# Copies of the key tail on ScalarE, and maxima joined from PSUM and kept positive

## The chip, the cores and the metric

One Trainium2 chip, one core of it. The metric is the device time of one execution in microseconds (us). Three runs of the kernel before gave 593.42, 593.97 and 594.81 us, median 593.97 us.

## What is computed

Attention over 4 batches with 8 heads of 576 tokens and 64 columns, with rotary embedding, then a soft mixture of experts on the result, then a dense layer pair. Only the attention matters here:

```python
q_rot, k_rot = (rotate(q), rotate(k))
scale = 1.0 / np.sqrt(D)
scores = scale * np.matmul(q_rot, k_rot.transpose(0, 1, 3, 2))
scores = scores - np.max(scores, axis=-1, keepdims=True)
attn = np.exp(scores)
attn = attn / (np.sum(attn, axis=-1, keepdims=True) + 1e-09)
return np.matmul(attn, v).astype(np.float32)
```

## The kernel before

The 32 heads are worked in 16 pairs, two heads of a pair on the two halves of the 128 partitions. For a pair, rotated k and q are split into a rounded part `hi` (ScalarE, L374) and a rest `lo` (GpSimd, L344), so that products of rounded numbers on TensorE can be added up to full precision. Keys go in four units of 128 and one last unit of 64 keys; the queries go in two halves of 288.

Each pair takes these steps. **Rotation** (`rope_pair`, L344) runs on GpSimd, six operations of 128x576, and on VectorE for the first pair alone. **Parts** (`parts_pair`): L374 and L344 again. **Windows** (`windows`, L418 and L422): the columns of the last 64 keys are copied from `hi` and `lo` into `wins`, so that the two query halves can share one 128-wide unit (`BOTH`). **Maxima** (`max_unit`): TensorE multiplies the rounded parts (L438) into a PSUM bank pair, VectorE takes the row maxima (L449); nine units a pair. **Joining** (`max_rows`): VectorE joins the unit maxima (L460), TensorE transposes them into PSUM (L465), VectorE writes them negated into the small tile `mr` in SBUF (L471), joins the two halves of `mr` in place (L476), and SP sends two rows by DMA into `mrows`. **Scores** (`st_unit`): TensorE adds three products of the parts (L504) and then the maxima, spread by the constant matrix `pick` (L511); ScalarE takes the exponential (L523); GpSimd adds two units (L531). **Values** (`pv_unit`): L551 and L546. **Sums** (`norm`): TensorE L572, then VectorE L578 to L596. **Logits** (`logits`): L638, L615, L620, with copies on ScalarE (L643, L650) and VectorE (L627, L629).

The steps of neighbouring pairs are interleaved: the maxima of pair p+1 are worked while the scores of pair p are. The order on each engine is made at build time by `Plan.emit`: each `op` has a due time, a cost per engine (the dictionary that comes first, as `{"DVE": 0.2}`), what it reads and writes, and the planner places the most urgent operation that can start. The engines then run their queues in that order, whatever the real durations are.

The maxima, scores, sums, logits and the transposed joined maxima all use one ring of three PSUM bank pairs (`bank_89`, `bank_90`, `bank_91` in listings of the order). An operation with `take="ring"` gets the bank pair that was freed longest ago; the one with `give="ring"` (made by `ring_op`) frees it. So TensorE can be at most three such steps ahead of VectorE and ScalarE. Before the change it is L471 that gives back the bank of the joined maxima.

`Plan.emit` also puts filler matmuls (L1524) where it expects TensorE to idle long; ten of them stand at the start, behind the first maxima.

After the attention come the experts and the dense pair; from about 377 us on TensorE works L1453 without a break.

Of the kernel before, what the change touches and what calls it, by code (L numbers as in the profile page):

```python
# [14 lines left out]
AF = mybir.ActivationFunctionType  # L15
ALU = mybir.AluOpType
# [3 lines left out]
B, H, S, D = 4, 8, 576, 64  # L20


T = dict(
    cpd=-10.26, wph=-19.05, wi0b=-82.9, wi1=0.41,
    wi2=15.39, wi3=-0.78, wp=-10.16, wp0=-1.88, wo0=0, wo1=7.84, wo=6.08, ahead=2.82, WAIT=0.51,
    lod=5.12, b0=1, nwarm=8, sprope=0.8, mxpe=1.14, mxdve=-0.4, stpe=0.22, stact=0.68, sums=-2.36, mrdve=1.0, smm=-0.48,
    norm=4.2, rope=-22.0, parts=-20.0, v=-5.6, lag=7.5, mr0=0.0, lgt=5.5, slots=6.0,
)
# [165 lines left out]
def kernel(  # L194
# [14 lines left out]
    nc = tc.nc  # L209
    plan = Plan()  # L210
    op = plan.op
# [8 lines left out]
    HQ = S // 2  # L220
# [7 lines left out]
    pick = pool.tile([128, 256], F32R, name="pick")  # L228
# [22 lines left out]
    keep_apart = pool.tile([10, 32], F32, name="keep_apart")[:, 0:1]  # L251
# [31 lines left out]
    def f(ap):  # L283
        return ap.bitcast(F32)
# [13 lines left out]
    def dma(fn, due, kb, reads=(), writes=(), after=None, on="SP", behind=None):  # L298
        return op({on: 0.5}, lambda e: fn(), due, reads, writes, kb=kb, after=after, behind=behind)


    def setup():
        nc.gpsimd.memset(ones, 1.0)
        nc.scalar.activation(out=nms[0], in_=ones[:, 0:1], func=AF.Exp)
        nc.gpsimd.memset(es, 0.0)
        nc.gpsimd.memset(f(pick), 0.0)
        for j in range(2):
            nc.gpsimd.memset(f(pick)[64 * j : 64 * j + 1, 64:192], 1.0)
        for h in his:
            nc.vector.memset(f(h)[:, :, S:], 0.0)  # L310
        for m in mrows:
            nc.vector.memset(f(m), 0.0)
        for x in los:
            nc.vector.memset(f(x[0])[:, S:], 0.0)
        nc.gpsimd.memset(f(wins), 0.0)
        nc.gpsimd.memset(half_ones, 0.0)
        for i in range(2):
            nc.gpsimd.memset(half_ones[64 * i : 64 * i + 64, i], 1.0)
            mcol, _ = small("mcol", [128, 2, 2, 5], bufs=2)
            nc.gpsimd.memset(mcol[:, 1, :, 4], -3e38)  # L320
# [81 lines left out]
    def on_ring(tok):  # L402
        return PAIRS[tok["slot"]]

    def ring_op(*args, **kw):
        i = op(*args, **kw)
        ring_ops.add(i)
        return i
# [4 lines left out]
    def windows(p, g):  # L413

        to = wins[:, 384 * (p % 2) : 384 * (p % 2) + 384].rearrange("p (i z n) -> p i z n", i=3, z=2)[:, :, 1]
        hi, lo = his[p % NHI], los[p % NLO][0]
        op(
            {"DVE": 0.2}, lambda e: nc.vector.tensor_copy(out=to[:, 0:2], in_=f(hi)[:, :, 512:S]),  # L418
            g, [("hi", p % NHI, t) for t in range(2)], [("win", p % 2, 0)],
        )  # L420
        op(
            {"DVE": 0.15}, lambda e: nc.vector.tensor_copy(out=to[:, 2], in_=f(lo)[:, 512:S]),  # L422
            g + 0.1, [("lo", p % NLO, 0)], [("win", p % 2, 1)],
        )

# [27 lines left out]
    def max_rows(p, g):  # L453
        mr, mrk = small("mrow", [10, 128], F32R, bufs=2)
        m10, m10k = small("m10", [128, 10])
        mcol, mk = mcols[p]
        tok = {}
        op(
            {"DVE": 0.15},
            lambda e: nc.vector.tensor_reduce(out=m10, in_=mcol.rearrange("p h j u -> p (j u) h"), op=ALU.max, axis=AX.X),  # L460
            g + T["mrdve"], [(mk, u, h) for u in range(5) for h in range(2 if u < BOTH else 1)], [m10k],
        )
        op(
            {"PE": 0.11},
            lambda e: nc.tensor.transpose(on_ring(tok)[0:10, 0, 0:128], m10, ident),  # L465
            g, [m10k, "ident"], [("rw", p)], take="ring", tok=tok, mode="f",
        )

        ring_op(
            {"DVE": 0.25},  # L470
            lambda e: nc.vector.tensor_scalar(out=mr, in0=on_ring(tok)[0:10, 0, 0:128], scalar1=-1.0, scalar2=None, op0=ALU.mult),  # L471
            g + T["mrdve"], [("rw", p)], [mrk], give="ring", tok=tok,
        )
        op(
            {"DVE": 0.2},
            lambda e: nc.vector.scalar_tensor_tensor(  # L476
                out=mr[:, 0:64], in0=f(mr)[:, 64:128], scalar=keep_apart, in1=f(mr)[:, 0:64], op0=ALU.add, op1=ALU.min
            ),
            g + T["mrdve"], ["apart"], [mrk],
        )  # L480
        for j in range(2):
            rows_done[p] = dma(
                lambda j=j: nc.sync.dma_start(out=f(mrows[p % 2])[64 * j : 64 * j + 1, :], in_=f(mr)[5 * j : 5 * j + 5, :]),
                g, 3, [mrk], [("mrow", p % 2, j)],
            )
# [71 lines left out]
    def norm(p, h, g):  # L557


        n = (2 * p + h) % 2  # L560
        acc, rest = accs[n], [p_slot(p, h, u) for u in (2, 3, BOTH)]
        tok = {}
        QUAD = [slice(32 * i, 32 * i + 32) for i in range(4)]

        def sums(e):
            sm = on_ring(tok)[:, 0]
            xs_ = [acc] + [x for x, _ in rest]
            for i in range(2):
                for j in range(2):
                    for w in range(2):  # L570
                        one = half_ones[:, h] if i and w else ones[:, 0:32]
                        nc.tensor.matmul(  # L572
                            sm[QUAD[2 * j + w], 0:HQ], lhsT=one, rhs=xs_[2 * i + w][:, j, :], start=(i == 0), stop=(i == 1)
                        )

        op({"PE": 0.97}, sums, g + T["sums"], [("acc", n)] + [k for _, k in rest], [("sm", n)], take="ring", tok=tok, mode="q")
        op(
            {"DVE": 0.42}, lambda e: nc.vector.transpose(out=on_ring(tok)[:, 1, 0:HQ], in_=on_ring(tok)[:, 0, 0:HQ]),  # L578
            g, [], [("sm", n)],
        )  # L580

        def inverse(e):
            col = on_ring(tok)[:, 1, 0:HQ].rearrange("p (b c) -> p b c", c=32)[:, :, 0:1]
            nc.vector.tensor_scalar(out=r9, in0=col, scalar1=1e-9, scalar2=None, op0=ALU.add)
            for q in range(4):
                nc.vector.tensor_tensor(out=r9[QUAD[q]], in0=r9[QUAD[q]], in1=col[QUAD[q ^ 1]], op=ALU.add)
            nc.vector.reciprocal(out=r9, in_=r9)

        ring_op({"DVE": 1.0}, inverse, g, [("sm", n)], ["r9"], give="ring", tok=tok)
        op(  # L590
            {"DVE": 0.42}, lambda e: nc.vector.transpose(out=recT, in_=r9.to_broadcast([128, HQ // 32, 32])),
            g, ["r9"], ["recT"],
        )
        op(
            {"DVE": 0.38},
            lambda e: nc.vector.tensor_tensor(out=xT[:, HALF[h]], in0=BANKS[6 + h][:, 0:HQ], in1=recT, op=ALU.mult),  # L596
            g, [("O", h), "recT"], [("xT", h)],
        )
# [200 lines left out]
    ring = {}  # L799
# [110 lines left out]
    def first_loads():  # L910
        for n, (what, s) in enumerate((("kq", 0), ("k", 1), ("rope", 0), ("rope", 1), ("k", 2), ("rope", 2), ("q", 1), ("q", 2))):
            rows, to, of = SEGS[s]
            q = "ACT" if s else "SP"
            if what == "rope":
                dst, src, keys = rope_sb[rows, :, to], rope[:, rows, of].rearrange("t r c -> r t c"), [("rope", t, s) for t in range(2)]
            else:
                ts_ = {"kq": slice(0, 4), "k": slice(0, 4, 2), "q": slice(1, 4, 2)}[what]
                dst, src, keys = raws[0][rows, ts_, to], qk[0][rows, ts_, of], [("raw", 0, t, s) for t in range(4)[ts_]]
            done = dma(
                lambda dst=dst, src=src, q=q: QUEUE[q].dma_start(out=dst, in_=src),  # L920
                -99 + 0.01 * n, (500 if what != "kq" else 1000) * (to.stop - to.start) / S, (), keys, on=q,
            )
        load(1, -35.5, slice(0, 4), "ACT", after=done, first="ACT")
        dma(lambda: nc.sync.dma_start(out=ident, in_=ident_in), -34, 65, (), ["ident"])

        def apart(e):
            nc.vector.tensor_tensor(out=keep_apart, in0=ident[0:10, 4:5], in1=ident[0:10, 9:10], op=ALU.add)
            nc.vector.tensor_scalar(out=keep_apart, in0=keep_apart, scalar1=-3e38, scalar2=3e38, op0=ALU.mult, op1=ALU.add)

        op({"DVE": 0.3}, apart, -20, ["ident"], ["apart"])  # L930

# [681 lines left out]
```

## Time and profile before

| what | value |
|---|---|
| median of three runs | 593.97 us |
| time of the profiled execution | 592.18 us |
| its span, first to last instruction | 590.4 us |
| TensorE (PE) busy | 562.1 us, 95% |
| VectorE (DVE) busy | 406.6 us, 69% |
| ScalarE (ACT) busy | 269.5 us, 46% |
| GpSimd (POOL) busy | 217.5 us, 37% |
| mean granted TensorE clock | 0.994 of full speed |

The profiled execution lies 1.8 us below the median of the runs; 1.78 us of its time lie outside of its span. PE's weight loads (PEld) run beside its matmuls, and its busy time is modelled from the starts. A row of a timeline is a start, a duration, the engine, the line, the operation, the tiles (written before `<-`, read after it) and how many; in brackets the idle time of the engine before it and what ended that.

### The profile page before, as it was taken

The page shows a single profiled execution, that of the slowest core. Times are in us where ns is not written, and L with a number is a line of the kernel's source. Part 1 is how long each engine was busy: PE and PEld are TensorE (multiplying, and loading weights), DVE is VectorE, ACT ScalarE, POOL GpSimd, SP SyncE. Part 2 cuts the span into 40 slices and gives each one's busy share as a digit, 9 for nine tenths or more (in the row PEclk, how much of TensorE's full clock was granted, in tenths as well). Part 3 has the DMA queues.
Part 4 walks back from the last instruction along what each step waited for, and adds up shares of the span by engine and source line. Part 5 has one row for each costly group of instructions (what it writes and reads, how often), then busy time and mean ns, then how long its engine had stood idle before and what let it go on. Part 6 is the DMA issues. An engine that isn't in the chain of part 4 may idle for free.

```text
span 590.4 us, 13397 instructions
## 1 busy us (share of the span) xinstructions
PE 562.1 (95%) x5519; PEld 423.3 (72%) x5519; DVE 406.6 (69%) x853; ACT 269.5 (46%) x475; POOL 217.5 (37%) x172
## 2 busy tenths in 40 slices
PE   1899999999999999999999899999999999999996
PEld 1756565566665666666754337999999999999996
DVE  3687887887787787777455458995594587535553
ACT  1234444444444443453432237876864465443440
POOL 1999999986879677721200000000000000000000
PEclk9799999999999999999999999999999999999999
DMA  9556775566367244036469998421400120000222
GB/s 188 120 124 164 185 193 148 152 175 169 100 174 210 54 100 105 24 95 227 154 226 378 386 392 330 143 81 64 144 1 1 60 84 2 1 1 1 108 108 107
DMA packets 36253, 80.90 MB, mean 137 GB/s; under 512 B 7616, under 2 KB 8032, under 8 KB 35168
## 3 DMA queue, kind: packets, MB, share of 16 engines
q1 hardware_dynamic: 34704, 77.98, 43.2%
q10 hardware_dynamic: 1488, 2.06, 1.8%
q8 instruction: 43, 0.70, 0.5%
q14 instruction: 18, 0.15, 0.1%
HBM read 75.24 MB, written 4.72 MB: 135 GB/s over the span
## 4 chain that ended last, share of the span: by engine, by line
PE 81%; DVE 11%; issue 2%; ACT 2%; DMA 1%; POOL 1%; ACTq 0%; DVEq 0%
PE bank L1453 32%; PE obank L551 11%; PE bank L504 10%; PE bank L572 5%; DVE mcol L449 5%; PE bank L438 4%; PE bank L511 3%; PE obank L1385 3%; PE bank L1239 2%; PE bank L638 2%; PE obank L546 2%; DMA arena<-in_rope_dram 1%; PE bank L1178 1%; PE bank L615 1%; POOL arena L344 1%
## 5 line engine op out<-in xcount | busy, mean ns | idle before, releaser
L523 ACT ACTIVATE tO<-bank 128x576 f32<-128x576 f32 x144 | 90.7, 650 | 114.3 <-PE bank L511 87.3
L344 POOL TENSOR_TENSOR arena<-arena 128x576 f32<-128x576 f32 x90 | 125.6, 1418 | 6.8 <-DMA arena<-in_qk_dram 6.2
L449 DVE TENSOR_REDUCE mcol<-bank 128x2 f32<-128x576 f32 x144 | 103.6, 747 | 14.5 <-PE bank L438 12.3
L1453 PE MATMUL bank<-w,tEb 128*128 128x256 f32 x864 | 106.1, 279 | 0.1
L1453 PEld LDWEIGHTS bank<-w,tEb 128*128 128x128 f32 x864 | 103.3, 188 | 2.3 <-issue 1.2
L551 PE MATMUL obank<-tO,pb 128*64 128x288 f32 x512 | 82.2, 424 | 0.0
L531 POOL TENSOR_TENSOR pb<-tO 128x576 f32<-128x576 f32 x32 | 45.2, 1413 | 51.0 <-ACT tO L523 50.9
L1453 PE MATMUL bank<-w,tEa 128*128 128x256 f32 x432 | 53.5, 279 | 0.0
L1453 PEld LDWEIGHTS bank<-w,tEa 128*128 128x128 f32 x432 | 51.9, 188 | 1.2 <-issue 0.8
L1453 PE MATMUL bank<-w,tO 128*128 128x256 f32 x432 | 51.3, 276 | 0.0
L1453 PEld LDWEIGHTS bank<-w,tO 128*128 128x128 f32 x432 | 50.9, 188 | 0.0
L551 PEld LDWEIGHTS obank<-tO,pb 128*64 128x64 f32 x512 | 28.6, 135 | 26.1 <-issue 16.9
L1396 ACT ACTIVATE pb<-obank 128x384 f32<-128x384 f32 x47 | 21.7, 493 | 42.9 <-PE obank L1385 42.9
L1396 ACT ACTIVATE arena<-obank 128x384 f32<-128x384 f32 x48 | 21.7, 494 | 36.2 <-PE obank L1385 36.1
L572 PE MATMUL bank<-tO,ones 128*32 128x288 f32 x256 | 36.5, 409 | 0.0
L504 PE MATMUL bank<-tEb 64*128 64x288 f32 x180 | 30.8, 339 | 1.4 <-DVE mcol L449 1.4
L438 PE MATMUL bank<-tEb 64*128 64x288 f32 x180 | 27.9, 337 | 2.4 <-DVE mcol L449 2.4
L344 POOL TENSOR_TENSOR tLb<-arena,tEb 128x576 fp32r<-128x576 f32 x20 | 28.2, 1420 | 3.1 <-ACT tEb L374 2.9
L504 PEld LDWEIGHTS bank<-tEb 64*128 64x128 f32 x180 | 16.9, 185 | 16.3 <-ACT tO L523 4.8
L1385 PE MATMUL obank<-x,tO 128*128 128x384 f32 x95 | 27.6, 345 | 0.8 <-DVE tO L1333 0.4
L578 DVE STREAM_TRANSPOSE bank<-bank 128x288 f32<-128x288 f32 x32 | 15.9, 498 | 17.5 <-PE bank L572 17.4
L438 PEld LDWEIGHTS bank<-tEb 64*128 64x128 f32 x180 | 15.8, 184 | 16.4 <-issue 8.6
(302 smaller groups left out, 1066.1 us busy)
## 6 DMA issues: line engine op xcount, KB each, us to landing
arena<-in_qk_dram SPq DMA_DIRECT2D x15, 576.0 KB
arena<-in_qk_dram SPq DMA_DIRECT2D x14, 512.0 KB
pb<-in_v_dram SPq DMA_DIRECT2D x16, 320.0 KB
arena<-in_w_dram SPq DMA_DIRECT2D x8, 512.0 KB
tLb<-in_w_in_dram SPq DMA_DIRECT2D x3, 1024.0 KB
pb<-in_w_in_dram SPq DMA_DIRECT2D x3, 1024.0 KB
w__440<-in_w_dram SPq DMA_DIRECT2D x4, 512.0 KB
w__652<-in_w_dram SPq DMA_DIRECT2D x4, 512.0 KB
```

Of the source, the lines that this page charges most:

```text
L344: ENG[e].tensor_tensor(out=o, in0=x, in1=y, op=how)
L438: nc.tensor.matmul(on_ring(tok)[:, j, 0:HQ], lhsT=x[rows], rhs=hi[rows, 0, HALF[c]], start=(u < BOTH or c == 0), stop=(u < BOTH or c == 1),)
L449: lambda e: nc.vector.tensor_reduce(out=mcol[:, h, :, u], in_=on_ring(tok)[:, :, 0:HQ], op=ALU.max, axis=AX.X),
L504: nc.tensor.matmul(st[:, j, 0:HQ], lhsT=w[rows], rhs=q[y][rows, HALF[c]], start=(i == 0 and (u < BOTH or c == 0)), stop=False,)
L511: nc.tensor.matmul(st[:, j, 0:HQ], lhsT=pick[rows, w : w + 128], rhs=mrow[rows, HALF[c]], start=False, stop=(u < BOTH or c == 1),)
L523: lambda e: nc.scalar.activation(out=pr, in_=on_ring(tok)[:, :, 0:HQ], func=AF.Exp, scale=0.125),
L531: lambda e: nc.gpsimd.tensor_tensor(out=acc, in0=one, in1=pr, op=ALU.add),
L551: nc.tensor.matmul(BANKS[6 + h][o, 0:HQ], lhsT=vr[:, u, j, :], rhs=pr[:, j, :], start=(h == 0 and u == 0), stop=(h == 1 and u == 3))
L572: nc.tensor.matmul(sm[QUAD[2 * j + w], 0:HQ], lhsT=one, rhs=xs_[2 * i + w][:, j, :], start=(i == 0), stop=(i == 1))
L1385: lambda e, i=i, t0=t0: nc.tensor.matmul(BANKS[i][:, 0:384], lhsT=wst_of()[:, 128 * fc : 128 * fc + 128], rhs=cst_of()[:, t0 : t0 + 384], ...
L1396: lambda e, i=i, h=h: nc.scalar.activation(out=rg_of()[:, 0, h], in_=BANKS[i][:, 0:384], func=AF.Relu),
L1453: nc.tensor.matmul(BANKS[c][:, z], lhsT=gt[:, x, 128 * c : 128 * c + 128], rhs=wo[:, fc % 2, y, z], start=(fc % FQ == 0 and i == 0 and z.s ...
```

## The change

Four edits, all in the attention:

1. The two copies of `windows` (L418, L422) go from VectorE to ScalarE, as activations with the function Copy.
2. In `max_rows`, L471 copies the transposed maxima times 1.0 where it was times -1.0, and L476 takes its first input from the PSUM bank where it was the SBUF tile `mr`; it joins by the larger (max) where it was by the smaller (min).
3. The bank of the joined maxima is given back by L476 where it was by L471.
4. Signs that follow: `pick` holds -1.0 where it was 1.0, and `keep_apart` swaps its two constants. The planner's cost of L578 is 0.45 where it was 0.42.

```diff
-            nc.gpsimd.memset(f(pick)[64 * j : 64 * j + 1, 64:192], 1.0)
+            nc.gpsimd.memset(f(pick)[64 * j : 64 * j + 1, 64:192], -1.0)
...
-            {"DVE": 0.2}, lambda e: nc.vector.tensor_copy(out=to[:, 0:2], in_=f(hi)[:, :, 512:S]),
+            {"ACT": 0.22}, lambda e: nc.scalar.activation(out=to[:, 0:2], in_=f(hi)[:, :, 512:S], func=AF.Copy),
...
-            {"DVE": 0.15}, lambda e: nc.vector.tensor_copy(out=to[:, 2], in_=f(lo)[:, 512:S]),
+            {"ACT": 0.18}, lambda e: nc.scalar.activation(out=to[:, 2], in_=f(lo)[:, 512:S], func=AF.Copy),
...
+        op(
+            {"DVE": 0.25},
+            lambda e: nc.vector.tensor_scalar(out=mr, in0=on_ring(tok)[0:10, 0, 0:128], scalar1=1.0, scalar2=None, op0=ALU.mult),
+            g + T["mrdve"], [("rw", p)], [mrk],
+        )
         ring_op(
-            {"DVE": 0.25},
-            lambda e: nc.vector.tensor_scalar(out=mr, in0=on_ring(tok)[0:10, 0, 0:128], scalar1=-1.0, scalar2=None, op0=ALU.mult),
-            g + T["mrdve"], [("rw", p)], [mrk], give="ring", tok=tok,
-        )
-        op(
             {"DVE": 0.2},
             lambda e: nc.vector.scalar_tensor_tensor(
-                out=mr[:, 0:64], in0=f(mr)[:, 64:128], scalar=keep_apart, in1=f(mr)[:, 0:64], op0=ALU.add, op1=ALU.min
+                out=mr[:, 0:64], in0=on_ring(tok)[0:10, 0, 64:128], scalar=keep_apart, in1=f(mr)[:, 0:64], op0=ALU.add, op1=ALU.max
             ),
-            g + T["mrdve"], ["apart"], [mrk],
+            g + T["mrdve"], ["apart", ("rw", p)], [mrk], give="ring", tok=tok,
         )
...
-            {"DVE": 0.42}, lambda e: nc.vector.transpose(out=on_ring(tok)[:, 1, 0:HQ], in_=on_ring(tok)[:, 0, 0:HQ]),
+            {"DVE": 0.45}, lambda e: nc.vector.transpose(out=on_ring(tok)[:, 1, 0:HQ], in_=on_ring(tok)[:, 0, 0:HQ]),
...
-            nc.vector.tensor_scalar(out=keep_apart, in0=keep_apart, scalar1=-3e38, scalar2=3e38, op0=ALU.mult, op1=ALU.add)
+            nc.vector.tensor_scalar(out=keep_apart, in0=keep_apart, scalar1=3e38, scalar2=-3e38, op0=ALU.mult, op1=ALU.add)
```

The planner orders the engines anew. With the bank numbers left out, TensorE's order stays as it was but for one stretch in the maxima of the second pair, where one block of four value matmuls is parted into two blocks of two; the whole attention has 237 runs of one kind of matmul where it had 235. GpSimd's order and SP's stay, and behind the attention everything does. What changes is at which of the three banks a step lands, and VectorE's and ScalarE's queues.

VectorE in the third pair's maxima, behind the first pair's reciprocal. Before:

```order
L587 RECIPROCAL r_87<-r_87 128x9
L449 TENSOR_REDUCE mcol_113<-bank_91 128x2
L449 TENSOR_REDUCE mcol_113<-bank_89 128x2
L449 TENSOR_REDUCE mcol_113<-bank_90 128x2
L418 CAST wins<-tEb 128x2x64
L449 TENSOR_REDUCE mcol_113<-bank_91 128x2
L591 STREAM_TRANSPOSE pb<-r_87 128x288
L596 TENSOR_TENSOR pb<-obank_92,pb 128x288
```

Of the change:

```order
L587 RECIPROCAL r_87<-r_87 128x9
L449 TENSOR_REDUCE mcol_113<-bank_89 128x2
L449 TENSOR_REDUCE mcol_113<-bank_91 128x2
L449 TENSOR_REDUCE mcol_113<-bank_90 128x2
L449 TENSOR_REDUCE mcol_113<-bank_89 128x2
L591 STREAM_TRANSPOSE pb<-r_87 128x288
L596 TENSOR_TENSOR pb<-obank_92,pb 128x288
```

The copy between the third and the fourth reduction is gone, and the four stand one behind the other.

ScalarE in the scores of a pair of the first batch (L523 are the exponentials, L643 and L650 copies of the logits step). Before:

```order
L523 ACTIVATE tO_81<-bank_91 128x576
L523 ACTIVATE tO_81<-bank_89 128x576
L523 ACTIVATE tO_81<-bank_90 128x576
L523 ACTIVATE tO_82<-bank_91 128x576 x2
L523 ACTIVATE tO_82<-bank_90 128x576
L643 ACTIVATE arena<-bank_89 128x4x128
```

Of the change:

```order
L523 ACTIVATE tO_81<-bank_91 128x576
L523 ACTIVATE tO_81<-bank_90 128x576
L523 ACTIVATE tO_82<-bank_89 128x576
L418 ACTIVATE wins<-tEb 128x2x64
L422 ACTIVATE wins<-tLb 128x64
L523 ACTIVATE tO_82<-bank_89 128x576
L523 ACTIVATE tO_82<-bank_90 128x576
L643 ACTIVATE arena<-bank_91 128x4x128
```

Both copies stand between two exponentials of the same pair.

TensorE from the transposed joined maxima (L465) to the next step on the same bank, in the seventh pair, of the change:

```order
L465 MATMUL bank_90<-ident,m_119 10x128
L638 MATMUL bank_89<-ident,pb 128x128 x4
L638 MATMUL bank_89<-ident,pb 64x128
L615 MATMUL bank_91<-pb,phi_sb 32x128 x4
L620 MATMUL bank_91<-pb,phi_sb 32x64 x4
L572 MATMUL bank_90<-pb,ones 32x288
```

Before it is the same row by row, with L638 on `bank_91` and L615 and L620 on `bank_89`: two steps stand between L465 and the sums L572, which take the bank that the joining gives back. VectorE's side of it, of the change (before, L476 reads `mrow_120` twice and not the bank):

```order
L460 TENSOR_REDUCE m_119<-mcol_116 128x10
L449 TENSOR_REDUCE mcol_113<-bank_89 128x2
L471 TENSOR_SCALAR mrow_120<-bank_90 10x128
L476 SCALAR_TENSOR_TENSOR mrow_120<-bank_90,keep_apart,mrow_120 10x64
```

The bank is free for L572 behind L476 where it was behind L471.

## Rows read from the trace of the kernel before

**Rows 1.** Busy time by stretches: start:end, length, busy us and instructions of each engine.
```profile
100.00:150.00 50.00, 49.40 (x572) 30.50 (x569) 40.96 (x102) 21.88 (x41) 41.50 (x31) 1.00 0.61 156
320.00:345.00 25.00, 23.03 (x192) 8.38 (x188) 10.70 (x45) 6.43 (x15) 0.00 (x0) 1.00 1.05 389
```

**Rows 2.** Waits of PE, 45 to 285 us: waiter <- waited for: total us, times, longest.
```profile
PE bank L438 <- DVE mcol L449: 1.5, 2, 1.1
PE bank L504 <- DVE mcol L449: 1.3, 6, 0.3
PE bank L638 <- DVE mcol L449: 0.6, 2, 0.3
PE bank L504 <- ACT tO L523: 0.2, 1, 0.2
```

**Rows 3.** Timeline, DVE and PE: one wait of PE and what stands before it.
```profile
69.35 1.40 DVE L422 CAST wins<-tLb 128x64 fp32r<-128x64 f32 x1
70.67 1.41 DVE L449 TENSOR_REDUCE mcol<-bank 128x2 f32<-128x576 f32 x2
71.57 0.40 PE L438 MATMUL bank<-tEb 64*128 64x288 f32 x2 [0.40 <-DVE mcol L449]
```

**Rows 4.** Timeline, POOL, DVE and PE around the joined maxima of the seventh pair.
```profile
128.00 1.41 POOL L531 TENSOR_TENSOR pb<-tO 128x576 f32<-128x576 f32 x1 [0.88 <-ACT tO L523]
128.11 0.28 DVE L471 TENSOR_SCALAR mrow<-bank 10x128 fp32r<-10x128 f32 x1 [0.19 <-PE bank L465]
128.42 1.07 DVE L476 SCALAR_TENSOR_TENSOR mrow<-mrow,keep_apart 10x64 fp32r<-10x64 f32 x1
129.02 0.41 PE L572 MATMUL bank<-pb,ones 128*32 128x288 f32 x1
```

**Rows 5.** Groups by line: shapes, count | busy us, mean ns | idle before.
```profile
L418 DVE CAST wins<-tEb 128x128 fp32r<-128x128 f32 x10 | 7.4, 743 | 4.3 <-ACT tEb L374 2.2 <-PE bank L504 2.1
L418 DVE CAST wins<-tEa 128x128 fp32r<-128x128 f32 x6 | 2.1, 356 | 0.9 <-ACT tEa L374 0.8
L422 DVE CAST wins<-tLb 128x64 fp32r<-128x64 f32 x10 | 7.4, 741 | 2.1 <-POOL tLb L344 2.1
L422 DVE CAST wins<-tLa 128x64 fp32r<-128x64 f32 x6 | 3.2, 534 | 0.0
L476 DVE SCALAR_TENSOR_TENSOR mrow<-mrow,keep_apart 10x64 fp32r<-10x64 f32 x16 | 15.0, 940 | 0.6
```

**Rows 6.** Timeline, PE: a maxima step and the scores behind it, without and with a wait.
```profile
121.36 0.29 PE L438 MATMUL bank<-tEa 64*128 64x288 f32 x2
121.56 0.40 PE L504 MATMUL bank<-tEb 64*128 64x288 f32 x2
...
125.84 0.33 PE L438 MATMUL bank<-tEb 64*128 64x288 f32 x2
126.43 0.40 PE L504 MATMUL bank<-tEb 64*128 64x288 f32 x2 [0.26 <-DVE mcol L449]
```

**Rows 7.** Timeline, PE: fillers and first scores at the start; a wait at 43.77.
```profile
23.63 3.20 PE L1524 MATMUL obank<-es 128*128 128x128 f32 x14
26.76 0.58 PE L504 MATMUL bank<-tEa 64*128 64x288 f32 x2
43.77 0.40 PE L438 MATMUL bank<-tEb 64*128 64x288 f32 x2 [0.88 <-DVE mcol L449]
```

**Rows 8.** One line's durations, min/median/max ns, first and last start.
```profile
L476 DVE SCALAR_TENSOR_TENSOR mrow<-mrow,keep_apart x16: 273/1064/1176, 24.2 to 283.7; 10x64 fp32r<-10x64 f32 x16
L596 DVE TENSOR_TENSOR pb<-obank,pb x32: 440/447/459, 47.4 to 303.5; 128x288 f32<-128x288 f32 x32
L650 ACT ACTIVATE arena<-bank x8: 257/258/258, 59.5 to 249.2; 64x128 f32<-64x128 f32 x8
```

**Rows 9.** Waits of the whole span.
```profile
ACT tO L523 <- PE bank L511: 87.3, 71, 3.9
PEld obank L551 <- issue: 16.9, 80, 0.4
```

## The prediction

> **What bounds the kernel now.** I read the busy time by stretches first. In the middle of the attention TensorE is busy 49.40 of 50 us and VectorE 40.96 [rows 1]. So TensorE is the bound, and whatever the change does to VectorE is worth only what TensorE idles for VectorE's sake. Next I read what PE waits for between 45 and 285 us, where the pairs run in their steady order: ten waits for the maxima's reduction L449, 1.5 + 1.3 + 0.6 = 3.4 us, and a single one of 0.2 us for an exponential [rows 2]. That is the whole of PE's idle time that another engine causes there. Then the timeline, for what stands before such a wait: at 69.35 a copy L422 of 64 columns takes 1.40 us on VectorE, two reductions follow, and PE, which has all three banks out, gets one back only at 71.57 and has idled 0.40 us [rows 3]. The reader should see that the copy is long, not that VectorE is full. Last, why it is long: L476, on only ten partitions, takes anything from 0.273 to 1.176 us with a median of 1.064 [rows 8], and the one at 128.42 ends at 129.49, 0.08 us behind the end of a GpSimd operation that began before it (128.00 + 1.41 = 129.41) [rows 4]. VectorE's instructions that work in SBUF alone are held until the GpSimd operation under way is over. GpSimd is busy 41.50 of the same 50 us [rows 1], so this is the rule and not the exception.
>
> **The change part by part.**
>
> *The copies leave VectorE.* Off its queue go 7.4 + 2.1 us of L418 and 7.4 + 3.2 us of L422, 20.1 us in 32 instructions, 0.63 us each [rows 5]. All of it lies beside TensorE's work; what shows is the waits. Each of the ten waits has a held copy before it in VectorE's queue, with at most two or three reductions between, as at 69.35, and each is shorter than what that copy takes (the longest wait, 1.1 us, lies behind the copy of the third pair whose removal the order shows). So I take all ten to go: 3.4 us by their brackets. The brackets count a little short, because ends of matmuls are modelled: from start to start, a maxima step and the scores behind it are 121.56 - 121.36 = 0.20 us apart without a wait, and 126.43 - 125.84 = 0.59 with one, so 0.39 were lost under a bracket of 0.26 [rows 6]. I add 0.1 us for each of the ten: **4.4 us** gained.
>
> *The waits that stay.* At 43.77 PE waits 0.88 us [rows 7] for the first of four reductions that stand behind the sums of the pair before; no copy stands ahead of them, and the order there is kept. This one stays, as do the waits in the first nine reductions, which come one behind the other with nothing between. At the very start the copies and L476 do stand on the way from the first maxima to the first scores, yet nothing comes of that: PE works fourteen filler passes from 23.63 to 26.83 and goes from them into the scores at 26.76 without a gap [rows 7], and the order keeps all these fillers. I take 0 here, with at most 0.5.
>
> *The joining reads PSUM.* The trace of before has no L476 of this form. Its bounds are 0.27 and 1.18 us, the shortest and the longest of the old form [rows 8]. The nearest row is L596, which also reads one PSUM bank and one SBUF tile: 0.440 to 0.459 us in all 32 cases, beside the same busy GpSimd [rows 8]. It is not held, so I take 0.28, the unheld form. That returns 15.0 - 16 x 0.28 = 10.5 us to VectorE [rows 5]. No wait of rows 2 needs it to go, so it adds nothing to the sum; it is a margin. The Trainium skill, "SBUF — State Buffer", section "Who interferes with whom", says that a VectorE instruction with at most one SBUF input and outside of the two-port modes does not contend with GpSimd, while copies in such modes and instructions with two SBUF inputs are locked out for a whole GpSimd instruction. By that rule the new L476 is free, as by the row of L596; were it held after all, the sum would be another, and that is the first rival.
>
> *The bank is held longer.* It now comes back behind L476: where L471 ends at 128.39, the bank would be free at about 128.42 + 0.28 = 128.70. The next step on it is L572 at 129.02 [rows 4], two steps later in the order. So there is 0.3 us of cover, and I cost this at nothing. If that cover is gone, each 0.1 us costs 1.5 us over fifteen pairs.
>
> *ScalarE gets the copies.* L650, 128 columns on 64 partitions, takes 0.258 us [rows 8]; for 128 and 64 columns I estimate 0.27 and 0.22, 16 x 0.49 = 7.8 us more on an engine that is busy 21.88 of 50 [rows 1]. No copy waits long for its input: the planner puts them behind the exponentials, well after GpSimd's part is done. But they stand between two exponentials, and an exponential mostly starts the moment its scores are there (ScalarE waited 87.3 us for L511 [rows 9]), so it can start up to 0.49 us late, and its bank comes back late. The bounds are 0 and 7.8 us. PE waited for an exponential once, for 0.2 us [rows 2], which says there is room. I take **0.2 us** lost.
>
> *One block more.* In the second pair a block of value matmuls is parted. Entering such a block cost PE's weight loads 16.9 us in 80 times, 0.21 us each [rows 9]; leaving it about as much at most. I take **0.2 us** lost, between 0.1 and 0.5.
>
> *Behind the attention* nothing is reordered. The weight loads that fill the DMA engines at 320 to 345 us (share 1.05) [rows 1] go into tiles that the attention gives back, so they start earlier by what the attention gains. I cost this at nothing.
>
> The sum is 4.4 - 0.2 - 0.2 = 4.0 us. The profiled execution took 592.18 us, so it would take 588.2. The median of the runs is 593.97, 1.8 us above, so I forecast **590.0 us**. About 0.2%, 1.2 us, is what a measurement of this kernel can tell from no change.
>
> **The rivals.**
>
> *Slower: L476 is still held, and now it holds a bank.* If reading one input from PSUM does not free it from GpSimd, it ends at 129.49 as now and the bank comes back then, 0.47 us behind the start of L572 [rows 4]. By the median at least eight of the sixteen are held that long [rows 8], and fifteen pairs have L572 on this bank: 8 x 0.47 = 3.8 to 15 x 0.47 = 7.1 us, say 5.5. Less the 4.0 gained, that is 1.5 us slower, 595.5 us. It decides from 4.0 / 15 = 0.27 us of wait for each pair. For it speaks that the constant and one input still come from SBUF; against it L596. Chance 0.07.
>
> *No change: the wait moves to ScalarE.* Where half of each pair's 0.49 us falls on the way of an exponential whose bank PE wants next, 16 x 0.25 = 4.0 us go back and the time stays at 594.0. For it: the copies stand in the middle of the exponentials, and with three banks each late one is felt. Against it: only one of PE's waits was for ScalarE. Also here belongs that the loads do not follow the attention and swallow the gain. The Trainium skill, "Perfetto Trace Analysis", section "Optimizing Scalar/DVE Operations", gives ScalarE the larger fixed cost on SBUF and advises such a move where VectorE is saturated. VectorE at 40.96 of 50 is not, so by that rule the time would stay as it is; the held copies before PE's waits speak against it here. Chance 0.12.
>
> *More than forecast.* With 30.6 us less on VectorE the reductions come earlier everywhere; if the wait of 0.88 at 43.77 and the short one behind it go too, and the start gives its 0.5, 2 us come on top: 588.0 us. Chance 0.13.
>
> **How the numbers follow.** The forecast, 588.8 to 592, has 0.68; more gain 0.13; no change 0.12; slower 0.07. Faster by over 0.2% are the forecast and the larger gain, and a little of the third case where it gives only part back: 0.82. Within 0.2%: 0.11. Slower: 0.07. The range leaves out the slower case and a little at either end: 587.0 to 593.3 us.
>
> **What would show it.** PE's waits for L449 between 45 and 285 us down from ten to two or fewer; L476 at 0.3 us in all sixteen cases; L418 and L422 on ScalarE at 0.2 to 0.3 us each; VectorE's busy time about 30 us less; the wait at 43.77 still there; TensorE's first scores still right behind the fillers. The forecast is wrong if PE's waits for L523 grow past 1 us, if L572 begins to wait for L476, or if the attention ends earlier and the end of the span does not follow.

## The result, and the profile after

The changed kernel takes **585.75 us** (median of 4 runs, 585.26 to 585.82); the kernel before, run beside it, takes 593.76 us (4 runs, 593.42 to 594.81). The ratio is 0.986, with a 95% interval from 0.9843 to 0.9878: 8.0 us faster. The forecast was 590.0 us in a range from 587.0 to 593.3. The direction was right, the gain was twice as large, and the time lies 1.25 us below the range.

| | before | after |
|---|---|---|
| profiled execution, us | 592.18 | 585.77 |
| its span, us | 590.4 | 584.0 |
| TensorE busy, us (share) | 562.1 (95%) | 558.9 (96%) |
| VectorE busy, us (share) | 406.6 (69%) | 381.4 (65%) |
| ScalarE busy, us | 269.5 | 275.6 |
| GpSimd busy, us | 217.5 | 217.2 |

The profiled execution after is a usual one: 585.77 us against a median of 585.75. The one before was 1.8 us below its median. So of the 8.0 us, 6.4 lie between the two profiles (592.18 - 585.77), and 1.6 do not.

First the waits of PE in the changed kernel, from 45 to 285 us (waiter <- waited for: total us, times, longest). This is the answer to [rows 2]:

```profile
PE bank L504 <- ACT tO L523: 0.5, 2, 0.2
```

All ten waits for L449 are gone. One wait of 0.2 us for an exponential was there before, a second has been added. Ahead of that stretch, from 30 to 45 us, two waits for L449 remain (they start at 43.43 and 44.10 us; the kernel before has them too, at 43.77 and 44.43):

```profile
PE bank L438 <- DVE mcol L449: 0.6, 1, 0.6
...
PE bank L504 <- DVE mcol L449: 0.3, 1, 0.3
```

The busy time by stretches, as [rows 1]. The columns are TensorE, its weight loads, VectorE, ScalarE, GpSimd, the granted clock, the DMA share and GB/s:

```profile
100.00:150.00 50.00, 50.00 (x586) 31.21 (x588) 36.11 (x93) 24.37 (x49) 43.11 (x32) 1.00 0.60 150
```

The profile shows no idle time of TensorE in the middle of the attention any more (50.00 of 50, before 49.40). VectorE falls from 40.96 to 36.11 and ScalarE rises from 21.88 to 24.37.

What the moved and rewritten operations take, by line (minimum/median/maximum in ns, first and last start), to be read against [rows 5, 8]:

```profile
L418 ACT ACTIVATE wins<-tEb x10: 299/301/317, 29.5 to 239.0; 128x128 fp32r<-128x128 f32 x10
L422 ACT ACTIVATE wins<-tLb x10: 245/246/257, 26.1 to 239.2; 128x64 fp32r<-128x64 f32 x10
L476 DVE SCALAR_TENSOR_TENSOR mrow<-bank,keep_apart,mrow x16: 271/272/273, 23.9 to 277.2; 10x64 fp32r<-10x64 f32 x16
```

No copy is held any more (the six of each line that read `tEa` and `tLa` take the same 0.30 and 0.25 us), and L476 takes 0.27 us in all sixteen pairs, where its median was 1.064. Around the joining of the seventh pair, the answer to [rows 4], GpSimd is again at work beside it (timeline: start us, duration us):

```profile
123.83 1.42 POOL L344 TENSOR_TENSOR arena<-arena 128x576 f32<-128x576 f32 x1 [2.07 <-DMA arena<-in_qk_dram]
123.87 0.28 DVE L471 TENSOR_SCALAR mrow<-bank 10x128 fp32r<-10x128 f32 x1 [0.63 <-PE bank L465]
124.18 0.27 DVE L476 SCALAR_TENSOR_TENSOR mrow<-bank,keep_apart,mrow 10x64 fp32r<-10x64 f32 x1
124.66 0.41 PE L572 MATMUL bank<-pb,ones 128*32 128x288 f32 x1
```

L476 runs from 124.18 to 124.45, in the middle of a GpSimd operation that lasts until 125.25, and it does not wait for it. The bank is back 0.2 us before L572 asks for it.

### The profile page after: what moved, and what is told of

Read it like the earlier page. It is cut to its first block, busy times and chain, and to the rows that moved or that the text cites. A ratio compares the mean times of both kernels' runs of the same rounds, so it can differ in the third digit from the quotient of the medians.

```text
span 584.0 us, 13391 instructions
## 1 busy us (share of the span) xinstructions
PE 558.9 (96%) x5519; PEld 422.3 (72%) x5519; DVE 381.4 (65%) x821; ACT 275.6 (47%) x507; POOL 217.2 (37%) x172
## 3 DMA queue, kind: packets, MB, share of 16 engines
q1 hardware_dynamic: 34704, 77.98, 44.1%
## 4 chain that ended last, share of the span: by engine, by line
PE 88%; DVE 6%; ACT 2%; DMA 2%; issue 1%; SPq 0%; ACTq 0%; DVEq 0%
PE bank L1453 32%; PE obank L551 13%; PE bank L504 12%; PE bank L572 6%; PE bank L438 5%; PE bank L511 3%; PE obank L1385 3%; PE obank L546 2%; PE bank L1239 2%; PE bank L638 2%; DMA arena<-in_rope_dram 1%; PE bank L1178 1%; PE bank L615 1%; DVE mcol L449 1%; PE bank L721 1%
## 5 line engine op out<-in xcount | busy, mean ns | idle before, releaser
L523 ACT ACTIVATE tO<-bank 128x576 f32<-128x576 f32 x144 | 90.8, 650 | 102.0 <-PE bank L511 80.3
L449 DVE TENSOR_REDUCE mcol<-bank 128x2 f32<-128x576 f32 x144 | 103.6, 748 | 27.4 <-PE bank L438 23.6
L572 PE MATMUL bank<-tO,ones 128*32 128x288 f32 x256 | 36.5, 409 | 0.0
L504 PE MATMUL bank<-tEb 64*128 64x288 f32 x180 | 30.5, 335 | 0.5 <-DVE mcol L449 0.3
L578 DVE STREAM_TRANSPOSE bank<-bank 128x288 f32<-128x288 f32 x32 | 15.9, 498 | 21.0 <-PE bank L572 20.8
L438 PE MATMUL bank<-tEb 64*128 64x288 f32 x180 | 28.0, 335 | 0.7 <-DVE mcol L449 0.6
L504 PEld LDWEIGHTS bank<-tEb 64*128 64x128 f32 x180 | 16.9, 185 | 14.5 <-issue 3.5
L438 PEld LDWEIGHTS bank<-tEb 64*128 64x128 f32 x180 | 15.9, 184 | 14.9 <-issue 8.9
```

The source lines that it names most:

```text
L438: nc.tensor.matmul(on_ring(tok)[:, j, 0:HQ], lhsT=x[rows], rhs=hi[rows, 0, HALF[c]], start=(u < BOTH or c == 0), stop=(u < BOTH or c == 1),)
L449: lambda e: nc.vector.tensor_reduce(out=mcol[:, h, :, u], in_=on_ring(tok)[:, :, 0:HQ], op=ALU.max, axis=AX.X),
L504: nc.tensor.matmul(st[:, j, 0:HQ], lhsT=w[rows], rhs=q[y][rows, HALF[c]], start=(i == 0 and (u < BOTH or c == 0)), stop=False,)
L523: lambda e: nc.scalar.activation(out=pr, in_=on_ring(tok)[:, :, 0:HQ], func=AF.Exp, scale=0.125),
L572: nc.tensor.matmul(sm[QUAD[2 * j + w], 0:HQ], lhsT=one, rhs=xs_[2 * i + w][:, j, :], start=(i == 0), stop=(i == 1))
```

## Where the gain lies in the two traces

I took the starts of the same matmuls in both traces (same line, same number in its order) and their difference, before minus after, along the time of before. Each step is a place where before lost time and after does not.

```
place (us, before)   waits of PE before      bracket   step of the difference
up to 43.8           L438, 0.88 to 0.64       0.24      0.3
47.0                 L438                     1.13      1.27, of which 0.6 is given back by 47.4, so 0.65
71.6 to 72.1         L438, L504               0.57      1.08
88.9                 L504 (under 0.1)         0.06      0.32
91.0                 L638                     0.30      0.69
108.7                L638                     0.31      0.61
126.4                L504                     0.26      0.54
177.0                L504                     0.26      0.61
212.4                L504                     0.17      0.41
229.5                L504                     0.27      0.51
246.5                L504                     0.15      0.39
small drifts between                                    0.3
after 250            none                               0; 6.4 in all, and 6.4 at the end
```

Two things are to be seen. Of the 6.4 us, 5.5 lie at the ten waits (a further stop, at 88.9, is too short for the list of waits), and after 250 us nothing is added or lost, so the end follows the attention. And the steps are larger than the brackets. Leaving out the wait at 47, the nine others have brackets of 2.29 us together, and their steps sum to 4.84: each costs its bracket **and 0.28 us more**, not 0.1.

The timeline shows why. First PE before, at the stop of 177 us:

```profile
176.33 0.40 PE L438 MATMUL bank<-tEb 64*128 64x288 f32 x2
176.99 0.40 PE L504 MATMUL bank<-tEb 64*128 64x288 f32 x2 [0.26 <-DVE mcol L449]
177.23 0.30 PE L504 MATMUL bank<-tLb,tEb 64*128 64x288 f32 x2
```

Then the same instructions after:

```profile
171.93 0.30 PE L438 MATMUL bank<-tEb 64*128 64x288 f32 x2
172.06 0.33 PE L504 MATMUL bank<-tEb 64*128 64x288 f32 x2
172.22 0.30 PE L504 MATMUL bank<-tLb,tEb 64*128 64x288 f32 x2
```

From start to start it is 0.13 and 0.16 us without a wait, and 0.66 and 0.24 us with one. The wait costs 0.53 + 0.08 = 0.61 us under a bracket of 0.26: the last matmul before the stop is shown longer (0.40 in place of 0.30 us) and the first behind it starts at a longer pitch. My pitch "without a wait" of 0.20 us [rows 6] was itself 0.07 us above the 0.13 here, so it took too little off.

What held the copies can be read in the trace of before itself. The copy of [rows 3], 69.35 to 70.75 us, stands beside this row of GpSimd, two operations of which the second ends at 70.70:

```profile
67.91 2.79 POOL L344 TENSOR_TENSOR arena<-arena 128x576 f32<-128x576 f32 x2
```

It is so wherever a copy is long. Of the 32 copies sixteen took over 0.5 us, and each of them ended 0.08 to 0.09 us (128 columns) or 0.05 to 0.06 us (64 columns) behind the end of a GpSimd operation; the other sixteen took 0.18 to 0.23 us. Of the sixteen L476, fifteen ended 0.075 to 0.077 us behind one, and the sixteenth, the one of 0.273 us, had no GpSimd operation beside it.

## The experiments

### The kernel before once more

What the difference of 1.6 us between the profile of before and its median is, could be asked of before itself: the same kernel, without an edit, profiled again.

> The kernel before, unchanged, profiled once more. The profiled execution that the forecast rested on took 592.18 us, 1.6 us below the median of the runs. Theory A (that execution was an easy one, and the usual one has longer waits of PE for L449): a profile at 593.5 to 594 us with about 1.5 us more of PE's waits behind held copies. Theory B (the offset lies outside of the attention, for instance in the granted clock or in the last stretch): the same waits, the attention as long as before, and the difference elsewhere.

It took 594.27 us (10 runs, 592.58 to 596.16), ratio 0.9999 [0.9979, 1.0018]; its profiled execution took 595.01. The waits of PE, 45 to 285 us:

```profile
PE bank L438 <- DVE mcol L449: 1.8, 4, 1.0
PE bank L504 <- DVE mcol L449: 1.7, 7, 0.3
PE bank L638 <- DVE mcol L449: 0.6, 2, 0.3
PE bank L504 <- ACT tO L523: 0.2, 1, 0.2
```

Thirteen waits for L449 in place of ten [rows 2]. By the matmuls' starts, what this execution loses against the first at stops around 159.7 and 176.3 us (times of the first) is 0.94 and 0.4 us. Something else adds 1.2 to 1.4 us at 47 to 50 us: the granted clock. The stretch from 47.2 to 50.7 us in the first profile of before:

```profile
47.20:50.70 3.50, 3.50 (x44) 2.08 (x46) 2.75 (x6) 1.22 (x2) 2.96 (x3) 1.00 1.03 200
```

and in this one:

```profile
47.20:50.70 3.50, 3.50 (x24) 2.03 (x28) 2.06 (x4) 1.22 (x2) 2.26 (x3) 0.51 1.06 206
```

A granted clock of 0.51 is the lower level, 1.2 GHz, for the whole stretch: 24 matmuls in its row in place of 44. What PE did before it fell was to wait at about 44 and for 1.0 us at about 46 to 47. So both theories have a part: longer waits, and the clock.

### The copies alone

```
-  {"DVE": 0.2}, lambda e: nc.vector.tensor_copy(out=to[:, 0:2], in_=f(hi)[:, :, 512:S]),
+  {"ACT": 0.22}, lambda e: nc.scalar.activation(out=to[:, 0:2], in_=f(hi)[:, :, 512:S], func=AF.Copy),
...
-  {"DVE": 0.15}, lambda e: nc.vector.tensor_copy(out=to[:, 2], in_=f(lo)[:, 512:S]),
+  {"ACT": 0.18}, lambda e: nc.scalar.activation(out=to[:, 2], in_=f(lo)[:, 512:S], func=AF.Copy),
```

> Only the two copies L418 and L422 go to ScalarE; the joining stays as before, in SBUF and held by GpSimd. Theory (what costs is a held copy ahead of a reduction for which PE waits; no wait of PE stands behind a held L476): nearly the whole gain, 7 to 8 us, 586 to 587 us, with PE's waits for L449 between 45 and 285 us at two or fewer. Rival (the gain goes with the time taken off VectorE, 20.1 of 30.6 us): 5.3 us, 588.5 us.

It took 586.88 us (6 runs, 586.19 to 587.86), ratio 0.9873 [0.9851, 0.9895]. The copies alone bring 7.2 us of the 8.0. The waits of PE, 45 to 285 us, and the joining, which is still the old form:

```profile
PE bank L504 <- ACT tO L523: 0.5, 2, 0.2
PE bank L504 <- DVE mcol L449: 0.3, 1, 0.3
```

```profile
L476 DVE SCALAR_TENSOR_TENSOR mrow<-mrow,keep_apart x16: 273/1065/1487, 23.8 to 278.0; 10x64 fp32r<-10x64 f32 x16
```

L476 is held as long as ever. The one wait for L449 in this list isn't one of the ten. It is the short one behind the wait at 43.77, which the kernel before has at 44.43, ahead of the stretch; here it reaches past 45 us:

```profile
44.65 0.40 PE L504 MATMUL bank<-tEb 64*128 64x288 f32 x2 [0.27 <-DVE mcol L449]
```

So all ten go with the copies alone: the copies were what stood before the reductions, and L476 hardly mattered.

### The joining alone

The changed kernel's lines 308, 469 to 479, 578 and 928, with the copies on VectorE as before.

> Only the joining of the maxima changes (read from PSUM, kept as maxima, bank given back behind it); the copies stay on VectorE. Theory: at most 1 us gained, 593 to 594 us, with the ten waits of PE for L449 still there. Rival (in proportion to VectorE's time, 10.5 of 30.6 us): 2.7 us gained, 591 us.

It took 592.54 us (12 runs, 591.21 to 597.03), ratio 0.9979 [0.9958, 0.9999]: 1.5 us, more than the 1 us expected and at the edge of what can be told from none. Its waits of PE, 45 to 285 us:

```profile
PE bank L438 <- DVE mcol L449: 1.5, 2, 1.1
PE bank L504 <- DVE mcol L449: 1.1, 5, 0.3
PE bank L638 <- DVE mcol L449: 0.3, 1, 0.3
...
```

Eight waits are listed in place of ten, some of them at other places, while L476 is at 0.271 to 0.273 us in all sixteen. The prediction had taken 0 for this part; a short stop or two is what it is worth. In this kernel L572 did wait for L476 once, 0.24 us at 39.5, so the cover over the bank is thin, but in the changed kernel it does not happen.

### The copies left on VectorE, in a form that is not held

This tells "VectorE has too much work" from "VectorE is held". The copies become reductions by maximum over an axis of length one: the same values, the same queue, the same order.

```
-  nc.vector.tensor_copy(out=to[:, 0:2], in_=f(hi)[:, :, 512:S])
+  nc.vector.tensor_reduce(out=to[:, 0:2], in_=f(hi)[:, :, 512:S].unsqueeze(3), op=ALU.max, axis=AX.X)
```

(and L422 likewise), once in the kernel before and once in the changed kernel.

> The kernel before in its own order; only the form of the two copies on VectorE changes: a maximum over an axis of length one, which writes the same numbers. If copies are held by GpSimd because of the form of a plain copy, this form should not be held: L418 and L422 at 0.2 to 0.35 us in all 32 cases, beside a GpSimd as busy as before. Theory (the hold is what costs): PE's waits go as with the copies on ScalarE, 586 to 588 us. Rival (VectorE simply has too much to do): 32 instructions of 0.25 us stay, 8 of 20.1 us, so some 3 of the 5.3 us. If the form is held too: no change, 593.8 us.

> The changed kernel with the copies back on VectorE, as maxima over an axis of length one (0.28 and 0.21 us, not held). Theory: 585.5 to 586.5 us, the changed kernel's time within 0.8 us, since nothing is held any more and 7.8 us of ScalarE are free. Rival (ScalarE is the better place, since VectorE's queue is the one for which PE waits): 587 us or more, with waits of PE for L449 back.

In the kernel before it gives 587.44 us (6 runs, 586.95 to 588.35), ratio 0.9882 [0.986, 0.9904]; in the changed kernel 586.13 us (6 runs, 585.52 to 589.94), ratio 0.988 [0.9854, 0.9906] to before, 0.4 us from the change itself, which cannot be told from none. The copies in the first of the two:

```profile
L418 DVE TENSOR_REDUCE wins<-tEb x10: 274/276/286, 29.9 to 239.6; 128x128 fp32r<-128x128 f32 x10
L422 DVE TENSOR_REDUCE wins<-tLb x10: 208/209/221, 26.3 to 241.2; 128x64 fp32r<-128x64 f32 x10
```

The copy of [rows 3] as a reduction, beside the same two GpSimd operations:

```profile
67.99 2.83 POOL L344 TENSOR_TENSOR arena<-arena 128x576 f32<-128x576 f32 x2
69.51 0.21 DVE L422 TENSOR_REDUCE wins<-tLb 128x64 fp32r<-128x64 f32 x1
```

The same data takes 0.21 and 0.28 us on the same engine beside the same GpSimd work, every time, where these copies took 0.74 on average [rows 5]. 6.7 us of the gain are to be had with nothing moved to ScalarE. So the holding was the cause, and ScalarE was only one way out of it. The Trainium skill, "SBUF — State Buffer", section "Who interferes with whom", says that copies and casts can enter the two-port modes and that a reduction on trn2 cannot; by that rule the reduction runs free, and the trace agrees, 0.206 to 0.287 us in all 32.

The waits of PE in these two kernels, 45 to 285 us, the first list from the kernel before, the second from the changed one:

```profile
PE bank L504 <- ACT tO L523: 0.4, 2, 0.2
PE bank L504 <- DVE mcol L449: 0.3, 1, 0.3
```

```profile
PE bank L504 <- ACT tO L523: 0.5, 2, 0.2
```

The wait for L449 is again the one at 44.43 of before, here at 45.17. And the second wait for an exponential, at 46.3 us in the changed kernel, is here too (at 47.43 and 46.24), with no copy on ScalarE. So it isn't the copies there that make it: it shows as soon as the long wait ahead of it is gone.

### One late operation, and fourteen

To measure the price of lateness by itself, a reduction of 1.34 us over 1,152 columns was put on VectorE of the changed kernel, ahead of the second set of maxima, once in the third pair and once in fourteen pairs. It writes two columns that nothing reads.

```
+    late = pool.tile([128, 2], F32, name="late")
...
+        if p == 2:
+            op(
+                {"DVE": 0.2},
+                lambda e: nc.vector.tensor_reduce(out=late, in_=f(hi)[:, :, 0:S], op=ALU.max, axis=AX.X),
+                g, [("hi", p % NHI, t) for t in range(2)], ["late"],
+            )
```

> The changed kernel with one more instruction on VectorE, a maximum over two times 576 columns of the third pair's rounded parts into a scratch tile that nothing reads, about 1.25 us, at the place between the third and the fourth reduction where the kernel before has the copy L418 at 44.96; TensorE's and ScalarE's orders are those of the changed kernel. Theory (one late reduction makes PE wait about 1 us, and that idle time is what lets the granted clock fall behind it): PE waits 0.9 to 1.1 us there, 0.7 to 1.3 us are lost, 586.5 to 587 us, and where the clock falls to 1.2 GHz for a stretch at 46 to 53 us another 1.4 us or more; times spread over 1 us or more. Rival A (a wait costs its bracket and no more, the clock does not depend on it): 0.6 us lost, all runs within 0.6 us. Rival B (the change gains by VectorE's total alone): 1.25 of 30.6 us, 0.3 us lost.

> The same instruction in the 14 pairs from the third on, 17.5 us on VectorE in all, not held by GpSimd. Theory (it is the time by which the reductions come late that costs, whatever makes the instruction long): most of the gain is gone, 591 to 595 us, with ten or more waits of PE for L449 between 45 and 285 us. Rival (the hold costs in another way, through GpSimd, which loses time to it): at most 588 us, since nothing is held here.

They took 593.5 us (12 runs, 592.9 to 594.89) and 597.67 us (6 runs, 596.57 to 599.99). Both are a miss: in the first the late operation cost 0.65 us where it stands, while some 6 us more were lost evenly in the last stretch, behind the attention, where nothing had been edited. The edit had a second effect: the new tile of 8 bytes takes 32 in the layout and moves every tile allotted behind it, among them the ten weight slots w0 to w9 that the last stretch reads. So both were made again with `late = xt[:, 352:354]`, two unused columns of an existing tile.

> The changed kernel with one reduction of 1.34 us put on VectorE ahead of the third pair's second set of maxima, as in the run with one late operation, but its result goes into columns of an existing tile that nothing reads, so that no tile of the program lies elsewhere. If the 6 us that the earlier run lost in its last stretch came from the new tile of 8 bytes, this one loses only what the late maxima cost: 0.6 to 1.3 us, 586.3 to 587.1 us; with a fall of the granted clock behind the wait, as in the second profile of the kernel before at 47.2 to 50.7 us, 1.4 us more. If the late operation itself was the cause, it comes out near 593 us again.

> The same operation in 14 pairs of heads, again without a tile of its own. If late maxima are what the kernel before paid for, at 0.4 to 0.6 us for each of ten waits and with a fall of the clock on top, this kernel lands at 590 to 593.5 us and its trace has waits of TensorE for L449 in most pairs. If the kernel before lost its time through the holding of VectorE in some other way than by lateness, 14 late operations cost little: 588 us or less.

They took 586.7 us (5 runs, 586.55 to 587.42) and **590.43 us** (6 runs, 590.07 to 591.83), that is 0.95 and 4.7 us above the changed kernel. The waits of PE with fourteen late operations, 45 to 285 us (lines lie 8 lower here: L446 is L438, L457 is L449, L512 is L504, L646 is L638):

```profile
PE bank L446 <- DVE mcol L457: 1.3, 2, 1.1
PE bank L446 <- DVE es L696: 1.2, 2, 0.6
PE bank L646 <- DVE mcol L457: 0.3, 1, 0.3
PE bank L512 <- DVE mcol L457: 0.2, 1, 0.2
PE bank L512 <- ACT tO L531: 0.2, 1, 0.2
```

The 590.43 us lie within what was expected, but the waits do not: fourteen late operations made six new stops and not one in most pairs (two of the six put down to L696, another operation of VectorE in the same queue); the other eight did not show. By the matmuls' starts, the five behind the first cost 0.59, 0.46, 0.34, 0.85 and 0.85 us under brackets of 0.31, 0.22, 0.24, 0.58 and 0.58: 3.09 against 1.93, or 0.23 us more than the bracket each. That is the same price as in before, made by hand. The first one, 1.1 us at 45 to 47, cost 0.7 us there, since PE no longer stops for the exponential behind it; then the clock went down:

```profile
47.20:50.70 3.50, 3.50 (x28) 1.34 (x24) 1.47 (x3) 1.22 (x2) 2.29 (x2) 0.55 1.07 201
```

### The tile alone

```
+    late = pool.tile([128, 2], F32, name="late")
...
+        nc.gpsimd.memset(late, 0.0)
```

> The changed kernel with only the tile of 8 bytes and no late operation (GpSimd clears it in the setup). If the tile shifts the operands of the last stretch's matmuls and that makes them slower, it lands at 591 to 593 us, the loss all between 381 and 590 us, with single matmuls of L1453 at 281 to 283 ns in place of 276 to 279. If the late operation was the cause of that loss, it stays within 0.5 us of the changed kernel, at 585.3 to 586.5 us.

> As the run with the 8-byte tile alone, but with a tile of 64 bytes. The small tile moved every tile allotted behind it, the weight slots w0 to w9 among them, by 32 bytes; this one moves them by 64, so that they lie to a multiple of 64 as in the changed kernel. If that remainder is what slows the matmuls of L1453, this kernel is back at 585.3 to 586.5 us; if any shift of these tiles does, or where a pair of tiles lies to each other, it stays at 592 to 593 us.

With 8 bytes 592.67 us (12 runs, 591.92 to 593.06), with 64 bytes 594.35 us (12 runs, 593.81 to 594.79): 6.9 and 8.6 us slower than the changed kernel for a tile that nothing uses. The groups of the last matrix product in the changed kernel (count, busy us, mean ns):

```profile
L1453 PE MATMUL bank<-w,tEb 128*128 128x256 f32 x864 | 106.1, 279 | 0.1
L1453 PE MATMUL bank<-w,tEa 128*128 128x256 f32 x432 | 53.5, 279 | 0.0
L1453 PE MATMUL bank<-w,tO 128*128 128x256 f32 x432 | 51.3, 276 | 0.0
```

with the tile of 8 bytes:

```profile
L1456 PE MATMUL bank<-w,tEb 128*128 128x256 f32 x864 | 109.6, 282 | 0.1
L1456 PE MATMUL bank<-w,tEa 128*128 128x256 f32 x432 | 55.1, 283 | 0.0
L1456 PE MATMUL bank<-w,tO 128*128 128x256 f32 x432 | 53.4, 281 | 0.0
```

and with that of 64 bytes (its first group):

```profile
L1456 PE MATMUL bank<-w,tEb 128*128 128x256 f32 x864 | 110.5, 284 | 0.1
```

The three groups sum to 210.9, 218.1 and 219.9 us: 7.2 and 9.0 us more, which is the whole loss. The two kernels with a late operation and the tile have 218.1 us there as well. The guess behind the second run, that the remainder by 64 bytes decides, fell: moved by 64 bytes the matmuls were slower still. What about the place makes the difference stays open. For this study it matters that the kernel before, the changed kernel and all runs without the tile have w0 to w9 at the same addresses and the same 210.7 to 210.9 us there, so their comparisons are clean.

## Why the prediction was right, and where it was wrong

*Ten waits go, nothing takes their place.* Right: ten to none, with one more wait of 0.2 us for an exponential.

*The copy before the reduction is the cause, and it is held by GpSimd.* Right. The copies alone bring 7.2 us, and freed on VectorE itself 6.7 us. But "VectorE's instructions that work in SBUF alone are held" is too wide: the copies as reductions work in SBUF alone too and were held in none of 32 cases. And "the rule and not the exception" holds for L476, fifteen of sixteen; of the copies it was half.

*The joining is a margin.* Nearly: 1.5 us alone, not 0; with the copies gone it adds about 1 us. The unheld form was right, 0.27 us against 0.28 taken.

*The price of a wait.* **This is the step that failed.** The mechanism was right and its size was not. The prediction put the ten waits at 4.4 us, 3.4 of brackets and "0.1 us for each of the ten". Measured, the nine smaller waits cost 0.28 us each above their brackets, and fourteen late operations made by hand show 0.23. Nine times 0.28 in place of 0.1 is 1.6 us more; 0.3 at 43.8, 0.3 at 88.9 and 0.3 in small drifts come on top, against 0.6 less at 47, where a wait for L523 of 0.24 us, hidden before behind the long one, took part back. 4.4 + 1.6 + 0.9 - 0.6 = 6.3, the 6.4 between the profiles but for rounding.

*The smaller costs.* The 0.4 us taken off for ScalarE and for the parted block do not show. The waits that L523 causes did grow, from 0.2 to 0.5 us, but they are 0.4 and 0.5 us with the copies on VectorE too. Ahead of the parted block the difference between the two traces is 0.08 us (at 31.4), behind it 0.07 (at 37.5). The copies take 0.30 and 0.25 us, not 0.27 and 0.22. VectorE's lines lose what was foretold, 20.2 us of copies and 10.6 of L476; its busy time fell by 25.2, since held copies and their neighbours overlap in the records.

*The median 1.8 us above the profile.* The prediction carried this offset over unchanged to the kernel after. That failed too, and it cost the range its lower end: the offset belonged to the waits. A second profile of before had three more stops and the lower clock at 47.2 to 50.7 us; 23 runs of before taken together spread over 3.7 us (592.38 to 596.05), the four of the changed kernel over 0.6. With the stops gone the offset went, 1.6 us. Where an unprofiled execution stopped cannot be seen, but its mean granted clock is on record. Of the 74 runs of before taken beside the experiments, 23 had 0.991 or less and took 595.2 us at the median; the other 51 took 593.5. Of the 46 runs of the six kernels without the wait of 1.1 us, a single one had 0.991. So the clock is a part of the offset; that the rest are stops that come and go is argued from the two profiles alone. Of the 4.25 us between forecast and result, 1.8 are this offset and 2.4 lie in the sum: the 1.6 of the price, the 0.9 at places that it put at nothing and the 0.4 taken off, less the 0.6 at 47, but for rounding.

*The rivals.* L476 held with a bank in hand: refuted by its sixteen durations. The wait moves to ScalarE: none of it, since the second wait for L523 is there with the copies on VectorE as well. The Trainium skill, "Perfetto Trace Analysis", section "Optimizing Scalar/DVE Operations", says that such a move may make sense where VectorE is saturated. It does not say that the move pays nothing elsewhere, as the prediction read it. VectorE was not saturated, with 40.96 of 50 us [rows 1], and the move alone still paid 7.2 us, so saturation is no condition for it here. "More than forecast", 588.0, came nearest, but for other reasons than it gave: the wait at 43.77 is still there, 0.64 us in place of 0.88, and the first scores came 0.3 us earlier (26.44 for 26.76), since the copy at 22.81 no longer stands ahead of the joining. A wait of 0.34 us for the values' transfer had taken all but 0.08 back by 30.5 us. So the prediction's 0 for the start was luck: the fillers moved with the scores and covered nothing.

## What to carry to other kernels

Ask how long the operation ahead of a late one takes at its longest, not how busy its engine is: VectorE's load was not the matter here, a held copy was, and writing the same copy as a reduction was worth nearly as much as moving it. Price a stop of a full TensorE by the distance from start to start against a place that is certainly free, which gave 0.2 to 0.3 us above the bracket, and give stops that come and go from one execution to the next their share in the median too. And before an extra tile in an experiment is taken for harmless, compare the stretches that it should not touch.

## What the runs showed of the hardware that I had not expected

**The clock can fall around a wait of 1.1 us.** Of the thirteen profiles, seven had the wait of 1.0 to 1.1 us for L449 at 45 to 47 us, and five of these had a granted clock of 0.50 to 0.70 between 47.2 and 50.7 us, which is the 1.2 GHz level for all or part of it. Of the six without that wait none had; all stood at 1.00. What PE had done before was much the same in all seven: idle for 0.6 to 0.9 us until 42.8 to 44.1, for 0.3 us more just behind, then busy for about 1.5 us, then idle for 1.0 to 1.1. The six had the first two of these stops as well. In the kernel with one late operation the fall cost about 0.9 us by the matmuls' starts (the difference went from 0.4 to 0.6 ahead of 47 us to 1.4 behind 50), and its execution with the fall, 587.42 us, is 0.6 us above the slowest of its other four (586.55 to 586.86). Its mean granted clock was 0.991, theirs 0.993 to 1.000. What decides between the five and the two is open, and that the wait is the cause is not shown beyond this count.

**Addresses decide over a per cent.** Weight slots moved by 32 or 64 bytes, with the small tiles that lie ahead of them, make the last product's 1,728 matmuls slower by 7.2 or 9.0 us (276 to 279 ns each became 281 to 284), with no wait in the list to show for it.
